# Gated linear-attention and local-attention block: KV^T in two 64-column array tiles, W2 = KV·Wo in 32x32 array tiles

## The chip, the cores and the metric

One NeuronCore of one Trainium2 chip. The metric is the device time of one execution in microseconds (us), median over several executions. PE is TensorE, PEld its loads of weights, DVE is VectorE, ACT is ScalarE, SP is SyncE, and PSUM is the memory, in banks, that matmuls write to. The chain of a profile is the work that ended last, followed back step by step to what each step had waited for.

## The reference, cut to what matters

```python
# S = 2048 tokens, D = 1024, H = 32 heads of Dh = 32; everything bf16
g = sigmoid((x * gate_w).sum(-1, keepdims=True))
# branch A, linear attention
q, k, v = split_heads(x @ A_wqkv)
pq, pk  = phi(q), phi(k)                       # phi(t) = where(t > 0, t + 1, exp(t)) + 1e-6
kv  = einsum("bhsd,bhse->bhde", pk, v)         # one 32x32 matrix per head
z   = pk.sum(over s)
num = einsum("bhqd,bhde->bhqe", pq, kv)
o   = num / (einsum("bhqd,bhd->bhq", pq, z)[..., None] + 1e-6)
a   = merge_heads(o) @ A_wo
# branch B: dilated local attention with its own weights, cut
return g * a + (1 - g) * b
```

Only the block-diagonal part of the 1024x1024 matrix KV is wanted: 32 blocks of 32x32, one per head. Since `a` is linear in `kv`, the kernel multiplies KV into Wo once (it calls the product W2), and then needs one matmul chain per row tile instead of two.

## The kernel before

Stages, with their matmuls on PE: pk = phi(x Wk) (`pk_ps`); G = x^T pk (`g_ps`); KV^T = Wv^T G (`kv_ps`); W2 = KV Wo, interleaved with V of branch B (both `p_ps`); V and q of branch A, row tile by row tile ("V/qA stage"); k and q of branch B with the local attention in between (`kq_ps`, `s`, `oB`); output (`d_ps`).

The parts that the change touches (cuts marked):

```python
# bdmask: 128x128, ones in the four diagonal 32x32 blocks
for c in range(KT):                              # 8 chunks of 128 columns = 4 heads each
    kvp = ps_1.tile([P, P], F32, name="kv_ps", tag="p1")
    for kt in range(KT):
        nc.tensor.matmul(kvp[:], lhsT=WvA[c // 4][:, kt, (c % 4) * P:(c % 4 + 1) * P],
                         rhs=G[c // 4][:, kt, (c % 4) * P:(c % 4 + 1) * P],
                         start=(kt == 0), stop=(kt == KT - 1))
    nc.vector.tensor_tensor(out=KVT[:, c, :], in0=kvp[:], in1=bdmask[:], op=ALU.mult)
# ...
def w2_event(c):                                 # two full-array matmuls per chunk
    def go():
        for half in range(2):
            w2p = bank1()                        # one of six PSUM banks
            nc.tensor.matmul(w2p[:], lhsT=KVT[:, c, :], rhs=WoA[half][:, c, :], start=True, stop=True)
            if half:
                nc.scalar.copy(out=WoA[half][:, c, :], in_=w2p[:])
            else:
                nc.vector.tensor_copy(out=WoA[half][:, c, :], in_=w2p[:])
    return go
# ... the end of normalize(t, pq, pn, prod), once per row tile of 128 tokens:
nc.vector.tensor_scalar(out=den[:], in0=den[:], scalar1=1e-6, scalar2=None, op0=ALU.add)
nc.vector.reciprocal(out=den[:], in_=den[:])
nc.vector.scalar_tensor_tensor(                  # pn = pq * ratio * (1/den), 1024 columns
    out=pn.rearrange("p (h e) -> p h e", h=H), in0=pq.rearrange("p (h e) -> p h e", h=H),
    scalar=ratio[:, t:t + 1], in1=den[:].rearrange("p (h o) -> p h o", o=1).broadcast_to([P, H, Dh]),
    op0=ALU.mult, op1=ALU.mult)
# ... V matmuls of the first four row tiles, with the W2 pairs put between them:
units = [u for t in range(4) for u in v_units(t)]
interleave(units, [(4 + 8 * c, w2_event(c)) for c in range(KT)])
```

Of each 128x128 product `kvp` only the four diagonal 32x32 blocks are used, a quarter; and in W2 three quarters of each weight matrix are zeros.

The softmax here doesn't subtract the row's maximum and nothing guards it: scores larger than these inputs give would overflow.

Of the kernel before, what the change touches and what calls it, by code (L numbers as in the profile page):

```python
# [9 lines left out]
ALU = mybir.AluOpType  # L10
BF16 = mybir.dt.bfloat16
F32 = mybir.dt.float32
PE = mybir.EngineType.PE
DVE = mybir.EngineType.DVE
P = 128
# [14 lines left out]
def interleave(units, events):  # L30

    events = sorted(events, key=lambda e: e[0])
    for i, unit in enumerate(units):
        while events and events[0][0] <= i:
            events.pop(0)[1]()
        unit()
    for _, fn in events:
        fn()
# [3 lines left out]
def kernel(  # L42
# [11 lines left out]
    nc = tc.nc  # L54
    S, D = A_x.shape[1:]
# [8 lines left out]
    H = 32  # L64
    Dh = D // H
    KT = D // P
# [5 lines left out]
    consts = ctx.enter_context(tc.tile_pool(name="consts", bufs=1))  # L72
    wpool = ctx.enter_context(tc.tile_pool(name="wpool", bufs=2))
# [5 lines left out]
    def load_w(name, src, col0, tag, only=(0, 1)):  # L79
        halves = []  # L80
        for h in only:
            w = wpool.tile([P, KT, 512], BF16, name=f"{name}{h}", tag=tag)
            c0 = col0 + h * 512
            nc.sync.dma_start(out=w[:], in_=src[:, c0:c0 + 512].rearrange("(kt p) n -> p kt n", p=P))
            halves.append(w)
        return halves
# [9 lines left out]
    for i in range(4):  # L96
        if i == 2:
            nc.sync.dma_start_transpose(out=xT[:, :, P:2 * P], in_=rows(x, P, 2 * P))
        nc.sync.dma_start(out=WkA[0][:, 2 * i:2 * i + 2, :],  # L99
                          in_=A_wqkv[2 * i * P:(2 * i + 2) * P, D:D + 512].rearrange("(kt p) n -> p kt n", p=P))  # L100
# [6 lines left out]
    WvA = load_w("WvA", A_wqkv, 2 * D, "wb")  # L107
    WoA = load_w("WoA", A_wo, 0, "wo")
# [3 lines left out]

    onesb = consts.tile([P, P], BF16, name="onesb")
    nc.vector.memset(onesb[:], 1.0)
    bdmask = consts.tile([P, P], F32, name="bdmask")
    nc.vector.memset(bdmask[:], 0.0)
    for i in range(4):
        nc.vector.memset(bdmask[32 * i:32 * i + 32, 32 * i:32 * i + 32], 1.0)


    def band(dst, lead):
# [11 lines left out]
    ratio = consts.tile([P, NB], F32, name="ratio")  # L133
    omg = consts.tile([P, NB], F32, name="omg")
    zrow = consts.tile([P, D], F32, name="zrow")
    KVT = consts.tile([P, KT, P], BF16, name="KVT")

    work = ctx.enter_context(tc.tile_pool(name="work", bufs=3))
    small3 = ctx.enter_context(tc.tile_pool(name="small3", bufs=2))
# [1 line left out]
    def phi(dst, pj):  # L141
        e = work.tile([P, 512], F32, name="e", tag="e")
        nc.scalar.activation(out=e[:], in_=pj[:], func=ACT.Exp)  # L143
        nc.vector.tensor_scalar(out=e[:], in0=e[:], scalar1=1.0, scalar2=1e-6, op0=ALU.min, op1=ALU.add)  # L144
        nc.vector.scalar_tensor_tensor(out=dst, in0=pj[:], scalar=0.0, in1=e[:], op0=ALU.max, op1=ALU.add)

    with tc.manual_schedule(engines={PE}):

        with ExitStack() as s1:
            ps_1 = s1.enter_context(tc.tile_pool(name="ps_1", bufs=6, space=bass.MemoryType.PSUM))  # L150
# [37 lines left out]
            for t in range(1, NB):  # L188
                side.append(lambda t=t: nc.vector.tensor_tensor(
                    out=zacc[:], in0=zacc[:] if t > 1 else pk[:, 0, :], in1=pk[:, t, :], op=ALU.add))  # L190
            side.append(lambda: nc.gpsimd.partition_all_reduce(zrow[:], zacc[:], P, bass_isa.ReduceOp.add))
            for t in range(NB):
                side.append(lambda t=t: nc.vector.tensor_tensor_reduce(
                    out=gjunk[:], in0=xrow[:, t, :], in1=gw_row[:], scale=1.0, scalar=0.0, op0=ALU.mult,
                    op1=ALU.add, accum_out=gdot[:, t:t + 1]))

            G = []
            for half in range(2):
                g_ = kq.tile([P, KT, 512], BF16, name=f"G{half}", tag="kq")
                G.append(g_)  # L200
                for kt in range(KT):
                    pj = ps_1.tile([P, 512], F32, name="g_ps", tag="p1")
                    for t in range(NB):
                        nc.tensor.matmul(pj[:], lhsT=xrow[:, t, kt * P:(kt + 1) * P],  # L204
                                         rhs=pk[:, t, half * 512:(half + 1) * 512],
                                         start=(t == 0), stop=(t == NB - 1))
# [7 lines left out]
            nc.vector.tensor_scalar(out=omg[:], in0=ratio[:], scalar1=1.0, scalar2=None, op0=ALU.add)  # L214
            nc.vector.reciprocal(out=omg[:], in_=omg[:])

            for c in range(KT):
                kvp = ps_1.tile([P, P], F32, name="kv_ps", tag="p1")
                for kt in range(KT):
                    nc.tensor.matmul(kvp[:], lhsT=WvA[c // 4][:, kt, (c % 4) * P:(c % 4 + 1) * P],  # L220
                                     rhs=G[c // 4][:, kt, (c % 4) * P:(c % 4 + 1) * P],
                                     start=(kt == 0), stop=(kt == KT - 1))
                nc.vector.tensor_tensor(out=KVT[:, c, :], in0=kvp[:], in1=bdmask[:], op=ALU.mult)
            WkB = load_w("WkB", B_wqkv, D, "wb")


# [9 lines left out]
            def bank1():  # L236
                return ps_1.tile([P, 512], F32, name="p1_ps", tag="p1")

            def w2_event(c):
                def go():  # L240
                    for half in range(2):
                        w2p = bank1()
                        nc.tensor.matmul(w2p[:], lhsT=KVT[:, c, :], rhs=WoA[half][:, c, :], start=True, stop=True)  # L243
                        if half:
                            nc.scalar.copy(out=WoA[half][:, c, :], in_=w2p[:])
                        else:
                            nc.vector.tensor_copy(out=WoA[half][:, c, :], in_=w2p[:])
                return go

            def v_units(t):  # L250
                def mm(half, kt, st):
                    if kt == 0:
                        st["pj"] = bank1()
                    nc.tensor.matmul(st["pj"][:], lhsT=xT[:, kt, t * P:(t + 1) * P], rhs=WvB[half][:, kt, :],  # L254
                                     start=(kt == 0), stop=(kt == KT - 1))
                    if kt < KT - 1:
                        return
                    v = Vst[t % 2]
                    nc.scalar.copy(out=v[:, half * 16:(half + 1) * 16, 0:Dh],
                                   in_=st["pj"][:].rearrange("p (h e) -> p h e", h=16))  # L260
                    if half == 1:
                        par, j = divmod(t, 8)

                        n = 128 - 16 * j
                        nc.sync.dma_start(out=V[16 * j:128, par * 9 + j], in_=v[0:n])
                        nc.sync.dma_start(out=V[0:16 * (j + 1), par * 9 + j + 1], in_=v[128 - 16 * (j + 1):128])
                for half in range(2):
                    st = {}
                    for kt in range(KT):
                        yield lambda half=half, kt=kt, st=st: mm(half, kt, st)  # L270

            def normalize(t, pq, pn, prod):
                nc.vector.tensor_tensor(out=prod, in0=pq, in1=zrow[:], op=ALU.mult)
                den = small3.tile([P, H], F32, name="den", tag="den")
                nc.vector.tensor_reduce(out=den[:], in_=prod.rearrange("p (h e) -> p h e", h=H),
                                        axis=mybir.AxisListType.X, op=ALU.add)
                nc.vector.tensor_scalar(out=den[:], in0=den[:], scalar1=1e-6, scalar2=None, op0=ALU.add)
                nc.vector.reciprocal(out=den[:], in_=den[:])
                nc.vector.scalar_tensor_tensor(
                    out=pn.rearrange("p (h e) -> p h e", h=H), in0=pq.rearrange("p (h e) -> p h e", h=H),  # L280
                    scalar=ratio[:, t:t + 1], in1=den[:].rearrange("p (h o) -> p h o", o=1).broadcast_to([P, H, Dh]),
                    op0=ALU.mult, op1=ALU.mult)

            def qa_units(t, bank, evacuate):
                def mm(half, kt, st):
# [11 lines left out]
            def qa_finish(t, half, pj):  # L297
                pq, pn = tmp[:, 4 + t % 2, :], tmp[:, 6 + t % 2, :]
                phi(pq[:, half * 512:(half + 1) * 512], pj)
                if half == 1:  # L300
                    normalize(t, pq, pn, prods[t % 2])
                    nc.sync.dma_start(out=pqd[t * P:(t + 1) * P, :], in_=pn)

            units = [u for t in range(4) for u in v_units(t)]
            interleave(units, [(4 + 8 * c, w2_event(c)) for c in range(KT)])
            for t in range(12):
                for u in v_units(4 + t):
                    u()
# [5 lines left out]
        with ExitStack() as s2:  # L314
# [102 lines left out]
            WoB = load_w("WoB", B_wo, 0, "wb")  # L417
            raw = wpool.tile([P, 4, D], BF16, name="raw", tag="wc")
            fw = wpool.tile([P, 2, D], F32, name="fw", tag="wc")
            pqT = [kq.tile([P, KT, 512], BF16, name="pqT0", tag="kq")]  # L420
            for t in range(4):
                nc.sync.dma_start_transpose(out=pqT[0][:, :, t * P:(t + 1) * P], in_=pqd[t * P:(t + 1) * P, :])
# [4 lines left out]
            def qa_late(t):  # L427
                r = raw[:, t - 12, :]
                for half in range(2):
                    h = slice(half * 512, (half + 1) * 512)  # L430
                    phi(r[:, h], r[:, h])
                normalize(t, r, r, fw[:, t % 2, :])
                nc.sync.dma_start_transpose(out=pqT[1][:, :, (t - 4) * P:(t - 3) * P], in_=r)

            def out_units(tb, bank):
                def mm(c0, n, side, c, st):
# [72 lines left out]
```

## Time and profile before

| | before |
|---|---|
| time, median of 3 runs | 491.4 us (491.37 to 491.46) |
| PE busy | 484.8 of 490.9 us |
| DVE busy | 279.1 us |
| KV^T and W2 on the chain | 3.57 and 3.45 us |

The page of the profile: busy time of the engines, and the chain of waits that ended last, by engine.

```profile
PE 484.8 (99%) x3332; PEld 230.5 (47%) x3332; DVE 279.1 (57%) x512; ACT 188.4 (38%) x283; POOL 16.0 (3%) x33
...
PE 98%; DMA 1%; SPq 0%; ACT 0%; issue 0%; ACTq 0%
```

So PE is what everything waits for, and only PE time counts unless another engine starts to hold it back. The next fence is that chain in order of time: start in us, length in us, engine, tile and line, and how many instructions were merged.

```profile
7.99 56.25 PE pk_ps L156 x252
64.24 55.25 PE g_ps L204 x256
119.49 3.57 PE kv_ps L220 x64
123.07 0.86 PE p_ps L254 x4
123.93 0.43 PE p_ps L243 x2
124.36 1.73 PE p_ps L254 x8
...
223.21 14.46 PE kq_ps L331 x67
```

Read three things here. KV^T (L220) is 64 matmuls in 3.57 us, 55.8 ns each. W2 (L243) is a pair of 512-column matmuls in 0.43 us, 216 ns each, eight times over: 3.45 us. And the next 512-column matmul always starts when the last one's column stream ends. From the start of KV^T to the first `kq_ps` matmul are 223.21 - 119.49 = 103.72 us; I call this **the stretch**: everything the change touches on PE before the output stage lies in it.

DVE in the V/qA stage, from the timeline (start, length, engine, line, operation, count, and in brackets the idle time before it and who ended it):

```profile
152.28 1.28 DVE L279 SCALAR_TENSOR_TENSOR tmp<-tmp,ratio,den 128x1024 bf16<-128x1024 bf16 x1
153.49 0.42 DVE L144 TENSOR_SCALAR e<-e 128x512 f32<-128x512 f32 x1
153.94 0.69 DVE L145 SCALAR_TENSOR_TENSOR tmp<-p_ps,e 128x512 bf16<-128x512 f32 x1
154.81 0.43 DVE L144 TENSOR_SCALAR e<-e 128x512 f32<-128x512 f32 x1 [0.18 <-ACT e L143]
```

L279 takes 1.21 us from its start to the next start, and there is one idle gap of about 0.2 us in each row tile of 6.9 us: DVE is nearly as full as PE in this stage.

### The profile page before, as it was taken

The page shows a single profiled execution, that of the slowest core. Times are in us where ns is not written, and L with a number is a line of the kernel's source. Part 1 is how long each engine was busy: PE and PEld are TensorE (multiplying, and loading weights), DVE is VectorE, ACT ScalarE, POOL GpSimd, SP SyncE. Part 2 cuts the span into 40 slices and gives each one's busy share as a digit, 9 for nine tenths or more (in the row PEclk, how much of TensorE's full clock was granted, in tenths as well). Part 3 has the DMA queues.
Part 4 walks back from the last instruction along what each step waited for, and adds up shares of the span by engine and source line. Part 5 has one row for each costly group of instructions (what it writes and reads, how often), then busy time and mean ns, then how long its engine had stood idle before and what let it go on. Part 6 is the DMA issues. An engine that isn't in the chain of part 4 may idle for free.

```text
span 490.9 us, 8143 instructions
## 1 busy us (share of the span) xinstructions
PE 484.8 (99%) x3332; PEld 230.5 (47%) x3332; DVE 279.1 (57%) x512; ACT 188.4 (38%) x283; POOL 16.0 (3%) x33
## 2 busy tenths in 40 slices
PE   7999999999999999999999999999999999999997
PEld 4444444446444444444445444445545444444444
DVE  0766689993328999997366666656655596000000
ACT  1333311111443333332566665666664332212121
POOL 3000000402000000000000000000000000000000
PEclk8999999999999999999999999999999999999999
DMA  8999960000621222236011151111163953111111
GB/s 193 153 276 371 348 224 0 0 1 5 216 62 61 91 95 88 63 125 196 3 30 37 32 115 30 30 36 29 37 151 81 212 87 85 33 43 33 43 34 43
DMA packets 80181, 46.56 MB, mean 95 GB/s; under 512 B 53520, under 2 KB 74128, under 8 KB 80144
## 3 DMA queue, kind: packets, MB, share of 16 engines
q1 hardware_dynamic: 80144, 46.04, 35.4%
q8 instruction: 26, 0.43, 0.4%
q14 instruction: 11, 0.09, 0.1%
HBM read 21.23 MB, written 7.34 MB: 58 GB/s over the span
## 4 chain that ended last, share of the span: by engine, by line
PE 98%; DMA 1%; SPq 0%; ACT 0%; issue 0%; ACTq 0%
PE kq_ps L331 23%; PE d_ps L444 21%; PE pk_ps L156 11%; PE g_ps L204 11%; PE p_ps L254 11%; PE p_ps L288 8%; PE q_ps L288 3%; PE oB L382 3%; PE s L357 2%; PE q_ps L444 1%; DMA xT<-in_A_x_dram 1%; PE kv_ps L220 1%; PE p_ps L243 1%; SPq L95 0%; SPq L99 0%; ACT osb L449 0%
## 5 line engine op out<-in xcount | busy, mean ns | idle before, releaser
L367 ACT ACTIVATE PT<-s 128x896 bf16<-128x896 f32 (+1 forms) x72 | 63.0, 926 | 24.5 <-PE s L357 24.5
L331 PE MATMUL kq_ps<-xT,WkB 128*128 128x512 bf16 x256 | 65.3, 379 | 0.0
L331 PE MATMUL kq_ps<-xT,WqB 128*128 128x512 bf16 x256 | 64.8, 379 | 0.0
L368 DVE TENSOR_TENSOR PT<-PT,mask 128x896 bf16<-128x896 bf16 (+1 forms) x72 | 44.7, 624 | 26.6 <-ACT PT L367 26.5
L156 PE MATMUL pk_ps<-WkA,xT 128*128 128x512 bf16 x256 | 57.4, 387 | 1.7 <-DMA WkA<-in_A_wqkv_dram 0.9
L254 PE MATMUL p_ps<-WvB,xT 128*128 128x512 bf16 x256 | 58.5, 379 | 0.0
L444 PE MATMUL d_ps<-WoA,pqT 128*128 128x512 bf16 (+1 forms) x248 | 56.9, 372 | 0.0
L444 PE MATMUL d_ps<-WoB,OBT 128*128 128x512 bf16 (+1 forms) x248 | 56.9, 372 | 0.0
L204 PE MATMUL g_ps<-pk,xrow 128*128 128x512 bf16 x256 | 55.4, 379 | 0.0
L144 DVE TENSOR_SCALAR e<-e 128x512 f32<-128x512 f32 x64 | 27.2, 425 | 43.5 <-ACT e L143 43.5
L449 ACT ACTIVATE osb<-d_ps,omg 128x512 bf16<-128x512 f32 (+1 forms) x31 | 20.9, 674 | 76.2 <-PE d_ps L444 76.1
L288 PE MATMUL p_ps<-WqA,xT 128*128 128x512 bf16 x192 | 43.4, 379 | 0.0
L156 PEld LDWEIGHTS <-xT 128*128 128x128 bf16 x256 | 25.5, 100 | 33.5 <-issue 3.5
L336 ACT CAST kqt<-kq_ps 128x512 bf16<-128x512 f32 x48 | 28.2, 588 | 31.8 <-PE kq_ps L331 31.6
L444 PEld LDWEIGHTS <-pqT 128*128 128x128 bf16 x264 | 25.8, 98 | 29.5
L444 PEld LDWEIGHTS <-OBT 128*128 128x128 bf16 x264 | 25.8, 98 | 29.3
L204 PEld LDWEIGHTS <-xrow 128*128 128x128 bf16 x256 | 25.0, 98 | 30.2
L254 PEld LDWEIGHTS <-xT 128*128 128x128 bf16 x256 | 25.0, 98 | 30.0
L288 PEld LDWEIGHTS <-xT 128*128 128x128 bf16 x256 | 24.3, 98 | 28.5
L143 ACT ACTIVATE e<-pk_ps 128x512 f32<-128x512 f32 x32 | 19.0, 597 | 43.8 <-PE pk_ps L156 43.8
L331 PEld LDWEIGHTS <-WqB 128*128 128x128 bf16 x256 | 23.0, 97 | 24.7
L331 PEld LDWEIGHTS <-WkB 128*128 128x128 bf16 x256 | 22.6, 97 | 24.1
(57 smaller groups left out, 400.3 us busy)
## 6 DMA issues: line engine op xcount, KB each, us to landing
xrow<-in_A_x_dram SPq DMA_DIRECT2D x4, 1024.0 KB, 12.7
out_dram<-osb SPq DMA_DIRECT2D x31, 128.0 KB, 1.9
pqd<-tmp SPq DMA_DIRECT2D x12, 256.0 KB, 2.1
WvA<-in_A_wqkv_dram SPq DMA_DIRECT2D x2, 1024.0 KB, 16.6
WoA<-in_A_wo_dram SPq DMA_DIRECT2D x2, 1024.0 KB, 13.7
WvB<-in_B_wqkv_dram SPq DMA_DIRECT2D x2, 1024.0 KB, 11.9
WqA<-in_A_wqkv_dram SPq DMA_DIRECT2D x2, 1024.0 KB, 10.0
WkB<-in_B_wqkv_dram SPq DMA_DIRECT2D x2, 1024.0 KB, 7.4
```

What stands on the lines that cost most here:

```text
L143: nc.scalar.activation(out=e[:], in_=pj[:], func=ACT.Exp)
L144: nc.vector.tensor_scalar(out=e[:], in0=e[:], scalar1=1.0, scalar2=1e-6, op0=ALU.min, op1=ALU.add)
L156: nc.tensor.matmul(pj[:], lhsT=xT[:, kt, t * P:(t + 1) * P], rhs=WkA[half][:, kt, :], start=(kt == 0), stop=(kt == KT - 1))
L204: nc.tensor.matmul(pj[:], lhsT=xrow[:, t, kt * P:(kt + 1) * P], rhs=pk[:, t, half * 512:(half + 1) * 512], start=(t == 0), stop=(t == NB - 1))
L254: nc.tensor.matmul(st["pj"][:], lhsT=xT[:, kt, t * P:(t + 1) * P], rhs=WvB[half][:, kt, :], start=(kt == 0), stop=(kt == KT - 1))
L288: nc.tensor.matmul(st["pj"][:], lhsT=xT[:, kt, t * P:(t + 1) * P], rhs=WqA[half][:, kt, :], start=(kt == 0), stop=(kt == KT - 1))
L331: nc.tensor.matmul(st["pj"][:], lhsT=W[c // 4][:, kt, (c % 4) * P:(c % 4 + 1) * P], rhs=xT[:, kt, cols], start=(kt == 0), stop=(kt == KT - 1))
L336: (nc.vector.tensor_copy if 0 <= after < 4 else nc.scalar.copy)(out=kqt[:, which, cols], in_=st["pj"][:])
L367: nc.scalar.activation(out=ptv[:, hs], in_=s4[:, hs, 0:W_], func=ACT.Exp, scale=SCALE)
L368: nc.vector.tensor_tensor(out=ptv[:, hs], in0=ptv[:, hs], in1=m[:, None, :].broadcast_to([P, 2, W_]), op=ALU.mult)
L444: nc.tensor.matmul(st["ps"][:, 0:n], lhsT=lhsT, rhs=W[c0 // 512][:, c, c0 % 512:c0 % 512 + n], start=(side == 0 and c == 0), stop=(side == ...
L449: nc.scalar.activation(out=osb[:, 0:n], in_=st["ps"][:, 0:n], func=ACT.Copy, scale=omg[:, tb:tb + 1])
```

## The change

The intent: use the array as several small ones, so that less of it works on blocks that are thrown away. KV^T is computed in two column tiles of 64 (two heads each), and no mask is needed. W2 is computed in passes of 16 matmuls, one per 32x32 tile of the array, each with 32 rows, 32 columns and a 512-column stream; row tile r writes to PSUM bank r, column tile j to its partitions 32j. So bank r of a pass gets head r of each of four chunks. The rows of W2 thus come out with the heads transposed within groups of four chunks, and `normalize` has to write `pn` in the same order.

```diff
-    KVT = consts.tile([P, KT, P], BF16, name="KVT")
+    KVT = consts.tile([P, KT, 64], BF16, name="KVT")
@@ KV^T
-            for c in range(KT):
-                kvp = ps_1.tile([P, P], F32, name="kv_ps", tag="p1")
-                ...  (64 matmuls of 128 columns, mask multiply)
+            for g in range(2):
+                kvp = ps_1.tile([P, 4, 64], F32, name="kv_ps", tag="p1")
+                for c in range(4):
+                    for kt in range(KT):
+                        for j in range(2):
+                            cols = slice(c * P + 64 * j, c * P + 64 * j + 64)
+                            nc.tensor.matmul(kvp[64 * j:64 * j + 64, c, :], lhsT=WvA[g][:, kt, cols],
+                                             rhs=G[g][:, kt, cols], start=(kt == 0), stop=(kt == KT - 1))
+                nc.vector.tensor_copy(out=KVT[:, 4 * g:4 * g + 4, :], in_=kvp[:])
@@ W2
-            def w2_event(c):  ...
+            def w2_event(g, half):
+                def go():
+                    w2p = [bank1() for _ in range(4)]
+                    for j in range(4):
+                        for r in range(4):
+                            rs = slice(32 * r, 32 * r + 32)
+                            nc.tensor.matmul(w2p[r][32 * j:32 * j + 32, :],
+                                             lhsT=KVT[rs, 4 * g + j, (r % 2) * 32:(r % 2) * 32 + 32],
+                                             rhs=WoA[half][rs, 4 * g + j, :], start=True, stop=True)
+                    for r in range(4):
+                        (nc.scalar.copy if r % 2 else nc.vector.tensor_copy)(
+                            out=WoA[half][:, 4 * g + r, :], in_=w2p[r][:])
@@ normalize
-                nc.vector.scalar_tensor_tensor(  ... 1024 columns, times ratio and 1/den)
+                nc.vector.tensor_scalar(out=den[:], in0=den[:], scalar1=ratio[:, t:t + 1], scalar2=None, op0=ALU.mult)
+                for g in range(2):
+                    nc.vector.tensor_tensor(
+                        out=pn[:, 512 * g:512 * g + 512].rearrange("p (r j e) -> p j r e", r=4, j=4),
+                        in0=pq[:, 512 * g:512 * g + 512].rearrange("p (j r e) -> p j r e", r=4, j=4),
+                        in1=den[...].broadcast_to([P, 4, 4, Dh]), op=ALU.mult)
@@ placing the passes
-            interleave(units, [(4 + 8 * c, w2_event(c)) for c in range(KT)])
+            interleave(units, [(8 + 12 * (2 * g + half), w2_event(g, half)) for g in range(2) for half in range(2)])
@@ (cut: the mask is gone; the four late row tiles write pn to a tile of their own instead of in place)
```

More of the change, by code (lines that the diff above doesn't have):

```diff
@@ L114 @@
     nc.vector.memset(onesb[:], 1.0)
-    bdmask = consts.tile([P, P], F32, name="bdmask")
-    nc.vector.memset(bdmask[:], 0.0)
-    for i in range(4):
-        nc.vector.memset(bdmask[32 * i:32 * i + 32, 32 * i:32 * i + 32], 1.0)
     def band(dst, lead):
@@ L215 @@
             nc.vector.reciprocal(out=omg[:], in_=omg[:])
-            for c in range(KT):
-                kvp = ps_1.tile([P, P], F32, name="kv_ps", tag="p1")
-                for kt in range(KT):
-                    nc.tensor.matmul(kvp[:], lhsT=WvA[c // 4][:, kt, (c % 4) * P:(c % 4 + 1) * P],
-                                     rhs=G[c // 4][:, kt, (c % 4) * P:(c % 4 + 1) * P],
-                                     start=(kt == 0), stop=(kt == KT - 1))
-                nc.vector.tensor_tensor(out=KVT[:, c, :], in0=kvp[:], in1=bdmask[:], op=ALU.mult)
+            for g in range(2):
[7 more added lines that the diff above has]
+                nc.vector.tensor_copy(out=KVT[:, 4 * g:4 * g + 4, :], in_=kvp[:])
             WkB = load_w("WkB", B_wqkv, D, "wb")
@@ L237, in bank1 @@
                 return ps_1.tile([P, 512], F32, name="p1_ps", tag="p1")
-            def w2_event(c):
+            def w2_event(g, half):
                 def go():
-                    for half in range(2):
-                        w2p = bank1()
-                        nc.tensor.matmul(w2p[:], lhsT=KVT[:, c, :], rhs=WoA[half][:, c, :], start=True, stop=True)
-                        if half:
-                            nc.scalar.copy(out=WoA[half][:, c, :], in_=w2p[:])
-                        else:
-                            nc.vector.tensor_copy(out=WoA[half][:, c, :], in_=w2p[:])
+                    w2p = [bank1() for _ in range(4)]
[8 more added lines that the diff above has]
+                            out=WoA[half][:, 4 * g + r, :], in_=w2p[r][:])
                 return go
@@ L278, in normalize @@
                 nc.vector.reciprocal(out=den[:], in_=den[:])
-                nc.vector.scalar_tensor_tensor(
-                    out=pn.rearrange("p (h e) -> p h e", h=H), in0=pq.rearrange("p (h e) -> p h e", h=H),
-                    scalar=ratio[:, t:t + 1], in1=den[:].rearrange("p (h o) -> p h o", o=1).broadcast_to([P, H, Dh]),
-                    op0=ALU.mult, op1=ALU.mult)
+                nc.vector.tensor_scalar(out=den[:], in0=den[:], scalar1=ratio[:, t:t + 1], scalar2=None, op0=ALU.mult)
[3 more added lines that the diff above has]
+                        in0=pq[:, 512 * g:512 * g + 512].rearrange("p (j r e) -> p j r e", r=4, j=4),
+                        in1=den[:, 16 * g:16 * g + 16].rearrange("p (j r o) -> p j r o", r=4, o=1)
+                        .broadcast_to([P, 4, 4, Dh]), op=ALU.mult)
             def qa_units(t, bank, evacuate):
@@ L419 @@
             fw = wpool.tile([P, 2, D], F32, name="fw", tag="wc")
+            lw = wpool.tile([P, 4, D], BF16, name="lw", tag="wa")
             pqT = [kq.tile([P, KT, 512], BF16, name="pqT0", tag="kq")]
@@ L431, in qa_late @@
                     phi(r[:, h], r[:, h])
-                normalize(t, r, r, fw[:, t % 2, :])
-                nc.sync.dma_start_transpose(out=pqT[1][:, :, (t - 4) * P:(t - 3) * P], in_=r)
+                pn = lw[:, t - 12, :]
+                normalize(t, r, pn, fw[:, t % 2, :])
+                nc.sync.dma_start_transpose(out=pqT[1][:, :, (t - 4) * P:(t - 3) * P], in_=pn)
             def out_units(tb, bank):
```

## The prediction

> **What bounds the kernel.** TensorE. The page shows PE busy 485 of 491 us, and the chain that ended last is 98% PE: in it one 512-column matmul follows the next every 0.216 us (16 in 3.45 us) without a gap from 8 us on. So the time changes by what the PE stream loses or gains, unless another engine starts to hold PE back.
>
> **What the change touches on PE.** KV^T: 64 matmuls of 128 columns, 3.57 us (chain, 119.5 to 123.1). W2: 16 matmuls of 512 columns, eight pairs of 0.43 us, 3.45 us (chain, 123.9 to 139.5). Together 7.0 us, 1.4% of the span, all on the chain: the ceiling of any gain.
>
> **After, estimated.**
> - W2: 4 passes of 16 matmuls on 32x32 tiles. Nearest in the trace is the scores group (32x128, four row tiles, 16 matmuls of 112 columns): 0.31 us in the chain for 16 x 47 ns of streaming, so four tiles do run at once; about 0.1 us of gap on each side I read as the cost of changing the tile mode. "TensorEngine Tiling (Array Packing)", Key Properties, says that changing the mode drains the engine, and that different tiles work in parallel. A pass then takes one stream (0.21 us), 15 issue steps of 5 to 15 ns and 0.2 us of switching: 0.5 to 0.6 us. Four: 2.1 us, a gain of 1.3 us.
> - KV^T: 128 matmuls of 64 columns in two column tiles: half the work, twice the instructions. The trace's small matmuls run at 20 ns (scores) to 25 ns (oB, 33 columns) each, weight load included: 128 at 20 to 27 ns is 2.6 to 3.5 us, plus a switch. The tiling page says that column tiling gives up fast weight load. [...]128 one after another 3.5 us. I take 3.2 us: a gain of 0.3 us, possibly a loss.
> - Sum: 7.0 to 5.3 us.
>
> **DVE.** normalize exchanges one 1.285 us operation (1.21 start to start) for a small scaling (0.2 us) and two 512-column multiplies of about 0.69 us each (estimate from 1.225 us for 1024 columns): +0.35 us for each of 16 row tiles. In the V/qA stage DVE idles only 0.2 us in each 6.9 us row tile (timeline), so it falls behind PE by about 0.15 us a row tile and ends the stage 1 to 2 us later. Six PSUM banks cover that, and its next work is 2.4 us later: PE should not notice. The four late row tiles run where DVE is mostly idle. The KVT copies are off the chain. The four banks of a pass are evacuated (2 x 0.69 DVE, 2 x 0.59 ACT, one V evacuation) within the 2.6 us to the next pass.
>
> **Prediction: 489.8 us, 488.8 to 491.6 (8 in 10).** Faster by over 2%: 1%. Within 2%: 98%. Slower: 1%.
>
> **What would show it.** In the chain: KV^T at 2.6 to 3.5 us; four W2 passes of 0.5 to 0.6 us; all later stages as long as before, 1 to 2 us earlier. On DVE: a new group of about 0.69 us, x32, and under 0.1 us of idle per row tile in the V/qA stage. No new PE wait on DVE or ACT.
>
> **What would make it wrong.** Column-tile weight loads that neither overlap nor run at the assumed rate (50 ns each: 6.4 us for KV^T, no gain, total about 493). The 16 tiles of a pass not running at once (four waves: 0.9 us a pass, no gain). The 4-dimensional multiply running slower than a plain one, so that DVE lags by more than the banks hold. A wait for banks at the passes.

## The result, and the profile after

| | before | after |
|---|---|---|
| time, median of 6 runs each | 491.38 us (490.72 to 492.78) | 488.53 us (487.95 to 489.80) |
| the stretch, from the chains | 103.72 us | 100.82 us |
| PE busy | 484.8 us | 480.5 us |
| DVE busy | 279.1 us | 281.0 us |

The ratio of the times is 0.9943, 95% interval 0.9924 to 0.9962 (the mean time of one kernel's fast runs over that of the other's of the same rounds, so not quite the ratio of the medians quoted). The gain of 2.85 us between the medians is clear of noise. The range ended at 488.8; the median lies 0.27 us below it. The prediction was wrong on the good side. That miss is small beside the spread of single runs (487.95 to 489.80 us); what shows that the sum behind the prediction was off is the stretch, 2.90 us shorter where 1.6 us had been predicted.

The chain after, the same columns:

```profile
8.69 53.74 PE pk_ps L152 x248
62.43 55.25 PE g_ps L200 x256
117.69 2.15 PE kv_ps L220 x128
119.83 1.83 PE p_ps L258 x8
121.66 0.36 PE p_ps L246 x16
122.03 2.70 PE p_ps L258 x12
...
218.51 14.46 PE kq_ps L339 x67
```

KV^T is down from 3.57 to 2.15 us although it has twice as many matmuls. A W2 pass takes 0.36 us for 16 matmuls, and there are four instead of eight pairs of 0.43. The V matmuls beside them (L258) became slightly longer: 8 take 1.83 us instead of 1.73, 12 take 2.70 instead of 2.59 (12 x 0.216). That is where a change of tile mode shows: about 0.11 us at each return to the full array. Going in costs nearly as much: by the single starts in the trace, 0.309 us lie between the last V matmul and the first tile of a pass, where the next full-array matmul would follow after 0.216. This 0.09 us is part of the 0.36 us of a pass. The whole account of the stretch: KV^T gains 1.42 us; from the end of KV^T to the first q matmul of branch A, 20.72 us (123.07 to 143.79) became 19.26 (119.83 to 139.09), 1.46 us less; together 2.88, and the stretch is 2.90 us shorter. What comes after is the same in both.

A warning about comparing the two spans: 490.9 and 486.2 us differ by 4.7, not by 2.9. The other 1.8 us lie before KV^T, in code that PE runs alike in both kernels: `g_ps` starts at 64.24 us in the one profile and at 62.43 in the other. Two experiments below that share this beginning with the changed kernel (kv_four32_split and kv_onetile) started `g_ps` at 62.33 and 64.34 us. The run of before that was profiled took 492.63 us, 1.25 above its kernel's median, and that of after 487.95 us, 0.58 below. So it is the chance of the start (in the slices of the page, the first slice of before had a granted clock of 8 tenths, after had 9), and part of the spread of about 2 us among the runs of one kernel. This is why I argue from the stretch and not from the span.

The groups of KV^T and W2 after, from the list of groups by line and shape (line, engine, operation, output<-inputs, shapes, count | busy us, mean ns of one | idle before):

```profile
L220 PE MATMUL kv_ps<-G,WvA 128*64 128x64 bf16 x128 | 2.2, 196 | 0.0
L246 PE MATMUL p_ps<-WoA,KVT 32*32 32x512 bf16 x64 | 1.7, 385 | 0.0
```

The length of one matmul (196 or 385 ns) is its latency, not its cost. The cost is the group's time in the chain over its count: 128 matmuls with their loads in 2.15 us are 16.8 ns each, or 33.6 ns for a pair, the change of mode at the start included. In the timeline a W2 pass is busy 0.43 us with matmuls of 0.385 us, so the 16 starts lie within 0.045 us: 3 ns apart. All 16 tiles stream at the same time. The Trainium skill, "TensorE: Matmul & The Clock Gate", Measured speedup vs the span model, gives about 4 ns per tile for this; the trace agrees.

DVE in the same place of the V/qA stage after:

```profile
154.43 0.24 DVE L284 TENSOR_SCALAR den<-den,ratio 128x32 f32<-128x32 f32 x1
154.70 1.29 DVE L286 TENSOR_TENSOR tmp<-tmp,den 128x512 bf16<-128x512 bf16 x2
155.91 0.42 DVE L140 TENSOR_SCALAR e<-e 128x512 f32<-128x512 f32 x1
156.37 0.69 DVE L141 SCALAR_TENSOR_TENSOR tmp<-p_ps,e 128x512 bf16<-128x512 f32 x1
157.02 0.43 DVE L140 TENSOR_SCALAR e<-e 128x512 f32<-128x512 f32 x1
```

The two multiplies of 512 columns take 1.21 us from start to next start, exactly as much as the one operation of 1024 columns before; the new cost is the small scaling, 0.27 us from start to start (154.43 to 154.70). The idle gap of 0.18 us is gone. DVE's last multiply of the stage ended 6.25 us after the first `kq_ps` matmul before (229.46 against 223.21), and 6.54 us after it now (225.05 against 218.51).

### The profile page after: what moved, and what is told of

Read it like the earlier page. It is cut to its first block, busy times and chain, and to the rows that moved or that the text cites. A ratio compares the mean times of both kernels' runs of the same rounds, so it can differ in the third digit from the quotient of the medians.

```text
span 486.2 us, 8390 instructions
## 1 busy us (share of the span) xinstructions
PE 480.5 (99%) x3444; PEld 227.0 (47%) x3444; DVE 281.0 (58%) x533; ACT 187.4 (39%) x283; POOL 15.9 (3%) x33
## 4 chain that ended last, share of the span: by engine, by line
PE 98%; DMA 1%; SPq 1%; ACT 0%; issue 0%; ACTq 0%
PE kq_ps L339 23%; PE d_ps L454 21%; PE p_ps L258 11%; PE g_ps L200 11%; PE pk_ps L152 11%; PE p_ps L296 9%; PE q_ps L296 3%; PE oB L390 3%; PE s L365 2%; PE q_ps L454 1%; DMA WkA<-in_A_wqkv_dram 1%; PE kv_ps L220 0%; PE p_ps L246 0%; SPq L95 0%; SPq L98 0%; SPq L99 0%
## 5 line engine op out<-in xcount | busy, mean ns | idle before, releaser
L258 PE MATMUL p_ps<-WvB,xT 128*128 128x512 bf16 x256 | 57.9, 379 | 0.0
L152 PE MATMUL pk_ps<-WkA,xT 128*128 128x512 bf16 x256 | 56.0, 379 | 1.3 <-DMA WkA<-in_A_wqkv_dram 0.8
L459 ACT ACTIVATE osb<-d_ps,omg 128x512 bf16<-128x512 f32 (+1 forms) x31 | 20.9, 673 | 76.5 <-PE d_ps L454 73.7
L152 PEld LDWEIGHTS <-xT 128*128 128x128 bf16 x256 | 24.9, 98 | 32.2 <-issue 1.6
L258 PEld LDWEIGHTS <-xT 128*128 128x128 bf16 x256 | 24.6, 98 | 30.0 <-issue 0.9
L296 PEld LDWEIGHTS <-xT 128*128 128x128 bf16 x256 | 24.3, 98 | 28.5
```

Source lines behind the costliest of these rows:

```text
L152: nc.tensor.matmul(pj[:], lhsT=xT[:, kt, t * P:(t + 1) * P], rhs=WkA[half][:, kt, :], start=(kt == 0), stop=(kt == KT - 1))
L258: nc.tensor.matmul(st["pj"][:], lhsT=xT[:, kt, t * P:(t + 1) * P], rhs=WvB[half][:, kt, :], start=(kt == 0), stop=(kt == KT - 1))
L296: nc.tensor.matmul(st["pj"][:], lhsT=xT[:, kt, t * P:(t + 1) * P], rhs=WqA[half][:, kt, :], start=(kt == 0), stop=(kt == KT - 1))
L459: nc.scalar.activation(out=osb[:, 0:n], in_=st["ps"][:, 0:n], func=ACT.Copy, scale=omg[:, tb:tb + 1])
```

## The experiments

Twelve kernels were run. The theory after the result: **A**, the gain is the sum of two independent parts on PE, KV^T and W2; KV^T is faster than predicted because the two column tiles load and stream at the same time. Rivals: **B**, most of the gain is W2 and the KV^T group only looks short; **C**, a matmul of 64 columns is simply cheap, whatever tile it is on; **D**, DVE holds PE back or releases it.

### The parts alone: kv_only, w2_only, norm_only, after_again

kv_only, KV^T alone, on the kernel before:

```diff
+    nc.vector.memset(KVT[:], 0.0)
@@ KV^T as in the change, but evacuated into the 128-wide block-diagonal KVT of before
+                for j in range(2):
+                    js = slice(64 * j, 64 * j + 64)
+                    nc.vector.tensor_tensor(out=KVT[js, 4 * g:4 * g + 4, js], in0=kvp[js],
+                                            in1=bdmask[js, None, js].broadcast_to([64, 4, 64]), op=ALU.mult)
```

> Undoes W2 and normalize, keeps the two 64-column tiles for KV^T (the block diagonal is cut out by the mask while evacuating). Theory A (the gain is the sum of two independent parts on PE): the KV^T group takes 2.15 us as in the changed kernel instead of 3.57, the stretch from the first KV^T matmul to the first kq_ps matmul is 1.4 us shorter than before (103.7 to 102.3), time about 490.0. Theory B (the gain is mostly W2, KV^T only looks short in the trace): the stretch stays within 0.5 us of 103.7.

w2_only, the changed kernel with the old KV^T:

```diff
@@ the 64 matmuls of 128 columns of before, then
+                for j in range(2):
+                    js = slice(64 * j, 64 * j + 64)
+                    nc.vector.tensor_copy(out=KVT[js, c, :], in_=kvp[js, js])
```

> Keeps the old 128x128 KV^T matmuls (3.57 us), with the new W2 passes and the new normalize. Theory A: each of the four passes costs 0.36 us plus about 0.12 us in the matmuls around it, the stretch from the first KV^T matmul to the first kq_ps matmul is 1.46 us shorter than before (103.7 to 102.3), time about 490.0. Theory B: about 2.4 us or more shorter.

norm_only, the new `normalize` (and the separate output tile of the late row tiles) put into the kernel before; nothing else.

> The new normalize (and its separate output tile) alone on the kernel before; the result is wrong on purpose, since the heads are transposed and W2 does not follow. DVE gets about 0.27 us more in each 6.9 us row tile. Theory A: PE does not notice, the stretch from KV^T to kq_ps stays at 103.7 us within 0.1 and the time is 491.4 within noise. Rival (DVE holds PE back): some us longer.

after_again is the changed kernel, unedited.

> The changed kernel again, as a control on the same chip: 2.85 us less than before in time (within 0.6), and 100.8 us from the first KV^T matmul to the first kq_ps matmul. If the 1.8 us that its first profile gained before the KV^T group (62.4 against 64.2 us at the start of g_ps) is chance, that start is not earlier in every profile.

Measured, on one chip, with the kernel before at 490.95 us (11 runs):

| kernel | time, 6 runs | ratio to before (95%) | stretch | against 103.72 |
|---|---|---|---|---|
| kv_only | 489.91 us | 0.9977 (0.9961 to 0.9994) | 102.40 us | -1.32 |
| w2_only | 489.99 us | 0.9977 (0.9960 to 0.9995) | 102.15 us | -1.57 |
| norm_only | 491.83 us | 1.0010 (0.9992 to 1.0028) | 103.72 us | 0.00 |
| after_again | 487.76 us | 0.9935 (0.9920 to 0.9951) | 100.82 us | -2.90 |

All but norm_only gave the reference's result. The chain of kv_only:

```profile
117.54 2.15 PE kv_ps L224 x128
119.68 0.97 PE p_ps L260 x4
...
219.94 14.46 PE kq_ps L337 x67
```

The chain of w2_only:

```profile
117.79 3.57 PE kv_ps L217 x64
121.36 1.73 PE p_ps L258 x8
123.09 0.37 PE p_ps L246 x16
...
219.94 14.46 PE kq_ps L339 x67
```

The chain of norm_only:

```profile
118.58 3.57 PE kv_ps L220 x64
...
222.30 14.46 PE kq_ps L334 x67
```

The parts add up: 1.32 + 1.57 = 2.89. Rival B falls: KV^T alone is worth nearly as much as W2. In kv_only the four V matmuls after KV^T take 0.97 us instead of 0.86, the 0.11 us of the change of mode; that is why 1.42 us in the group become 1.32 in the stretch, and it is also the 0.10 us by which the first V group of the changed kernel is longer, which I had booked to W2 above. Rival D falls for this change: `normalize` alone moves the stretch by nothing. The times of single kernels spread by about 2 us, so by times alone kv_only and w2_only are only just distinguishable from before.

### Why is a KV^T matmul so cheap: kv_serial, kv_full, kv_n32, kv_onetile

kv_serial: the two column tiles no longer alternate.

```diff
-                    for kt in range(KT):
-                        for j in range(2):
+                    for j in range(2):
+                        for kt in range(KT):
```

> The changed kernel with the two column tiles of KV^T no longer alternating: for each chunk all eight contraction steps of tile 0, then all eight of tile 1. Same 128 instructions. Theory A (the 16.8 ns per load and matmul come from two column tiles loading and streaming at the same time): consecutive matmuls now hit the same tile, so each costs one tile's own period, 27 to 34 ns, and the group takes 3.5 to 4.3 us instead of 2.15. Rival B (a 64-column load and matmul simply costs 17 ns, whichever tile): 2.15 us.

kv_full: the whole array as weights, 64 columns streamed, half of the output rows thrown away; two banks.

```diff
+                            nc.tensor.matmul(kvp[j][:, c, :], lhsT=WvA[g][:, kt, c * P:(c + 1) * P],
+                                             rhs=G[g][:, kt, cols], start=(kt == 0), stop=(kt == KT - 1))
```

> KV^T with 128 matmuls of 64 columns on the whole array (128-column weights, half of the rows of each result thrown away), no tiles. Theory A: no overlap of tiles, so 128 matmuls at 64 columns cost about 27 to 29 ns each (estimate: half of the 55.8 ns that the 128-column matmul took), 3.5 to 3.7 us. Rival B (fewer columns per matmul alone gives the gain): about 2.15 us.

kv_n32: 64-column weights as in the change, but only 32 columns streamed (the result is wrong).

> The changed kernel with only 32 of the 64 moving columns in each KV^T matmul, 64-column weights as before; the result is wrong on purpose. If a tile's period is set by its weight load, or by the issue of instructions, the group stays at 2.1 us; if it is set by the streaming of the 64 columns[...], it falls to about 1.3 us.

kv_onetile: the changed kernel's 128 matmuls, all on column tile 0.

```diff
-                            nc.tensor.matmul(kvp[64 * j:64 * j + 64, c, :], lhsT=WvA[g][:, kt, cols],
+                            nc.tensor.matmul(kvp[j][0:64, c, :], lhsT=WvA[g][:, kt, cols],
@@ and each half moved to its partitions by the copy
+                    nc.vector.tensor_copy(out=KVT[64 * j:64 * j + 64, 4 * g:4 * g + 4, :], in_=kvp[j][0:64])
```

> KV^T with the same 128 loads and matmuls (64 columns each), but all on the first column tile, into two banks; the second half is moved to its partitions when it is evacuated, so the result stays correct. In kv_serial tile 1 may still have started while tile 0 had matmuls waiting. If the 16.8 ns per matmul of the changed kernel needs the second tile: each matmul then costs one tile's own step, about 27 ns, the group 3.5 us. If not: about 2.2 to 2.7 us.

The KV^T line of the chain of each, in the order kv_serial, kv_full, kv_n32, kv_onetile:

```profile
117.86 2.67 PE kv_ps L220 x128
```

```profile
118.72 3.73 PE kv_ps L220 x128
```

```profile
117.47 2.13 PE kv_ps L221 x128
```

```profile
119.59 4.17 PE kv_ps L220 x128
```

| kernel (once each) | KV^T | per matmul | stretch | time |
|---|---|---|---|---|
| changed kernel, two tiles alternating | 2.15 us | 16.8 ns | 100.82 us | 487.76 us (median of 6) |
| kv_onetile, one tile | 4.17 us | 32.6 ns | 102.85 us | 491.86 us |
| kv_full, whole array | 3.73 us | 29.1 ns | 102.31 us | 490.45 us |
| kv_serial, one tile after the other | 2.67 us | 20.9 ns | 101.35 us | 488.62 us |
| kv_n32, half the stream | 2.13 us | 16.6 ns | 100.82 us | 487.71 us |

Only kv_n32 differed from the reference. kv_onetile began KV^T about 1.9 us later than the changed kernel (119.59 against 117.69 us); that is in its time, but not in its stretch. What follows:

- kv_onetile decides. One tile needs 32.6 ns for each load and matmul, somewhat more than the 27 ns expected; two tiles in turn need 33.6 ns for a **pair**. The second tile is as good as free. Rival C falls, and kv_full says the same in another way: 64-column matmuls on the whole array cost 29.1 ns each, so halving the columns alone would have gained nothing over the 3.57 us of before. Both kernels also write to two banks in turn, which the changed kernel does not. That is not what slows them: kv_serial's first matmuls, all on tile 0 and in one bank, start 31 to 32 ns apart (after a first gap of 53 ns), as they do in kv_onetile. And in the changed kernel the two matmuls of a pair start 3 ns apart, and the pairs 32 ns apart (single starts in the packed traces).
- kv_n32: half the stream changes nothing (2.13 us). So the 33 ns are not the streaming of 64 columns. They go with what stayed the same, the loading of 64 columns of weights and the tile's own turnaround; the run does not separate these two.
- kv_serial missed its expectation of 3.5 to 4.3 us: 20.9 ns is less than the 32.6 ns that one tile needs. So tile 1 must work beside tile 0 even when the program lists eight matmuls of one and then eight of the other. The single starts fit this: they read as series of eight, 31 to 32 ns apart, and a new series begins 5 to 6 ns after the fifth start of the one before it. (The trace does not name the tile of a matmul; this is read from the pattern.) Alternating is better, by 0.5 us, but not necessary for most of the overlap.

### More and smaller tiles: kv_four32 and kv_four32_split

If two column tiles overlap, four might too, and with 32 columns only the wanted blocks are computed. kv_four32:

```diff
-                        for j in range(2):
-                            cols = slice(c * P + 64 * j, c * P + 64 * j + 64)
-                            nc.tensor.matmul(kvp[64 * j:64 * j + 64, c, :], lhsT=WvA[g][:, kt, cols],
+                        for j in range(4):
+                            cols = slice(c * P + 32 * j, c * P + 32 * j + 32)
+                            nc.tensor.matmul(kvp[32 * j:32 * j + 32, c, :], lhsT=WvA[g][:, kt, cols],
```

> KV^T in four 32-column tiles, only the 32x32 diagonal blocks: 256 matmuls of 32 columns, correct result, KVT half as wide. If four tiles overlap as two do and only a tile's own load and stream count: 64 rounds of about 20 ns, 1.3 us, the kernel 0.85 us faster than the changed one, about 487.3 (at best a tie in time, shown by the trace). If there is a floor per instruction of 8 ns or more: 2.1 us or longer, no gain.

It was correct, and no gain: 491.01 us (6 runs, before 490.97 on the same chip; ratio 1.0005, 0.9987 to 1.0023), stretch 103.13 us. (The stretch is 2.3 us longer than that of the changed kernel, the median time 3.2 us; how long the pause was in the runs without a profile is not known.) Its chain:

```profile
117.90 1.65 PE kv_ps L220 x187
119.54 2.11 issue
121.65 0.70 PE kv_ps L220 x69
```

Two things went wrong. The 256 matmuls take 1.65 + 0.70 = 2.35 us, 9.2 ns each, so 37 ns for four tiles where I had hoped for 20. By the single starts, the first 32 matmuls run in rounds of four, about 25 ns a round after the first; from then on they start 8 to 9 ns apart, one by one, as in the other case that the expectation had named. What runs out there is not known. And in the middle PE stands still for 2.11 us, waiting for nothing that the profile shows ("issue"). In that window the DMA view has this row for 118 to 124 us, in kv_four32:

```profile
q8 instruction: 2, 0.03, 2.1%
```

and in the changed kernel for 117 to 124 us:

```profile
q8 instruction: 1, 0.02, 0.8%
```

These are blocks of instructions being fetched, 16 KB each. In the `g_ps` stage of kv_four32, where a matmul with its load comes every 0.216 us, one such fetch follows the other after 27.7 us, the time of 128 matmuls and 128 loads: so this queue feeds PE. In the trace of kv_four32 the first of the two starts at 119.30 us, 0.24 us before the pause; PE goes on at 121.65 us. The Trainium skill, "Runtime: NRT & Kernel Launch", Instruction fetch mechanics, says that each engine refills its instruction memory in blocks of 16 KiB, 256 instructions, and calls the cost mostly hidden. 256 matmuls with 256 loads are two such blocks, used up here in 2.35 us. So the theory: PE ran out of instructions. kv_four32_split puts eight V matmuls between the two halves:

```diff
-            for g in range(2): ...
+            def kv_group(g): ...
+            kv_group(0)
@@ second half after 8 V matmuls, the W2 passes 4 matmuls later than in the change
+            interleave(units, [(8, second_group)] + [(12 + 12 * (2 * g + half), w2_event(g, half)) for g in range(2) for half in range(2)])
```

> kv_four32 with its two halves (128 matmuls each) apart: eight V matmuls stand between them. kv_four32 stood still for 2.1 us in the middle of its 256 matmuls, 0.25 us after the fetch of one 16 KB block of instructions had begun. If PE had run out of instructions there: no such pause, and the two halves take 0.8 to 1.1 us each, 1.6 to 2.1 us together. If the pause belongs to something else in KV^T (the G or WvA tiles, the bank, the mode): it stays near 2 us.

Its chain:

```profile
117.58 1.12 PE kv_ps L220 x128
118.71 1.83 PE p_ps L258 x8
120.54 0.48 PE kv_ps L220 x51
121.03 0.37 issue
121.40 0.77 PE kv_ps L220 x77
```

The pause shrank from 2.11 to 0.37 us, with the same tiles, banks and matmuls, only thinned out; the halves take 1.12 and 1.25 us (a little over the expectation). (The edit also puts the load of WkB behind the second half, but it was issued at nearly the same time, 118.79 against 119.11 us.) Two numbers of the traces bind the pause to the fetch. PE stops after 187 matmuls counted from the start of KV^T in both kernels (128 + 8 + 51 in this one), so after as many instructions, though at another matmul of KV^T. And it goes on 2.35 us after the fetch began in kv_four32 (119.30 to 121.65) and 2.34 us in this one (119.06 to 121.40). The block itself had landed after 0.92 and 0.97 us; what the rest is spent on is not shown. This supports the instruction supply as the cause, and goes against the tiles, the bank or the mode; a direct record of PE waiting for its instructions is not in the trace, so I call it supported, not shown. One run, 488.55 us, correct: no better than the changed kernel, since 2.37 us of KV^T plus the pause is more than 2.15 (stretch 101.54 us against 100.82). So neither four-tile version beats the changed kernel.

### What a W2 pass costs: w2_split

Each pass is cut into two visits of 8 tiles (two of the four chunks), with four V matmuls between; same 64 matmuls.

```diff
-                    for j in range(4):
+                    for j in (2 * part, 2 * part + 1):
@@ copies after the second part; events at 8 + 12 * pass + 4 * part
```

> Each W2 pass of 16 tiles cut into two visits of 8 tiles with four V matmuls between. If a visit costs one 512-column stream plus the change of mode, however many of the 16 tiles it uses: eight visits of about 0.34 us plus 0.12 us, 3.7 us instead of 2.0, and the stretch from KV^T to kq_ps grows by about 1.7 us to 102.5. If the cost goes by matmuls: half per visit, no change (100.8).

Its chain:

```profile
121.97 0.34 PE p_ps L250 x8
122.30 0.97 PE p_ps L264 x4
```

A visit of 8 matmuls takes 0.34 us, one of 16 takes 0.36, and each return costs 0.11 us beside it. The stretch is 102.50 us (117.99 to 220.49), 1.68 us longer for four more visits, as expected. A pass costs its 512-column stream plus the change of mode, and the other tiles come nearly free. The run gave 489.92 us, once.

### How far is DVE from holding PE back: norm_heavy

The first product of `normalize` is done twice:

```diff
                 nc.vector.tensor_tensor(out=prod, in0=pq, in1=zrow[:], op=ALU.mult)
+                nc.vector.tensor_tensor(out=prod, in0=pq, in1=zrow[:], op=ALU.mult)
```

> The changed kernel with the first product of normalize done twice: 1.26 us more of DVE in each row tile, so that DVE needs about 8.1 us of work for 6.9 us of PE. It tests the claim that six banks cover a small lag of DVE and how far: after 12 row tiles DVE is about 14 us behind; the banks hold about 5 to 8 us. Expected: the V/qA stage (from the first W2 pass to the first kq_ps matmul) stretches by 6 to 10 us and the time rises to 494 to 499. If DVE did not matter at all for PE, 488.

The time was 495.06 us (once, correct), within the 494 to 499 expected, but not where I had put it, and partly by chance: its KV^T began at 119.32 us, 1.6 us later than in after_again (117.74). PE in the timeline:

```profile
217.98 3.61 PE L297 MATMUL p_ps<-WqA,xT 128*128 128x512 bf16 x16 [1.03 <-DVE tmp L141]
```

The first listed idle time of PE on DVE is 1.03 us before the last q group (by the starts, 0.26 us was lost at the q group before it); the whole stretch grew only by about 1.5 us, and the rest of the loss fell in the next stage, where `kq_ps` waited once for ACT (2.2 us) and once for DVE (1.5 us) by the view of who waited for whom. The banks and the end of the stage took up more lag than my 5 to 8 us. So the small extra DVE work of the change has room, as norm_only shows, but 1.26 us per row tile has not.

## Why the prediction was right or wrong

The prediction was wrong in size: 489.8 (488.8 to 491.6) against 488.53 us measured. Point by point:

1. **PE bounds the kernel, 7.0 us are the ceiling.** Right: the chain after is again 98% PE, and the gain in the stretch is 2.90 us.
2. **W2: "Four: 2.1 us, a gain of 1.3 us".** Nearly right. By w2_only the gain is 1.57 us, so W2 costs 3.45 - 1.57 = 1.88 us, 0.47 us a pass with its changes of mode, against the 0.5 to 0.6 predicted. The Trainium skill, "TensorEngine Tiling (Array Packing)", Key Properties, says that tiles work in parallel and that a change of mode drains the engine; the trace agrees with the first (3 ns between starts), and 0.09 us on going in and 0.11 us at a return fit the second.
3. **KV^T: "128 at 20 to 27 ns is 2.6 to 3.5 us", "128 one after another 3.5 us. I take 3.2 us".** This is the step that failed. The loads do not come one after another: they and the matmuls of the two column tiles run side by side, at 33.6 ns a pair (16.8 ns each), while one tile alone needs 32.6 ns for each (kv_onetile). The group took 2.15 us. The mis-sized term: 3.2 us against 2.15 us in the group, or 2.25 us with its return to the full array. Of the 1.3 us between the predicted gain (491.4 - 489.8 = 1.6) and the measured stretch (2.90), this term is about 1.0; W2 gives another 0.2, and the rest is rounding. I had cited that different tiles work in parallel, used it for W2, and then added up KV^T as if there were one tile; the lower bound of 20 ns came from a group of the trace that has no column tiles. A clause cut from the prediction read the weight loads of that group (the scores, on four row tiles) as 14 ns apart. That is busy time over count, 0.22 us over 16; the single starts lie 2 to 4 ns apart within each four. So loads that run side by side could already be seen in the trace of before. Whether column tiles give up fast weight load, as the prediction cites, no run here isolates.
4. **DVE "falls behind PE by about 0.15 us a row tile and ends the stage 1 to 2 us later".** Wrong in size, right in effect. The extra work was 0.27 us per row tile, not 0.35, because two multiplies of 512 columns cost 1.21 us start to start, as the one operation did; it filled the idle gap, and DVE ended the stage only 0.3 us later relative to PE. PE did not notice (norm_only: 0.00 us).
5. **"No new PE wait on DVE or ACT".** Right: no PE group of the changed kernel in the stretch shows idle time, and the waits for banks did not come.
6. **The range.** It reached down to a gain of 2.6 us. The two PE terms with their lower costs as I had bounded them (2.6 us for KV^T, 0.5 us a pass) would have given 7.0 - 4.6 = 2.4 us; the range ended where those bounds did, and the bound on KV^T was taken from groups of another shape.

## What to carry to other kernels

When a small matmul group is costed for array tiles, cost one round over all tiles (the load and turnaround of one tile), not the sum over the instructions, and add about 0.1 us for each change of mode, going in as well as coming back (0.09 and 0.11 us here). Collect as many tiles as possible into one visit, since a visit costs its stream whether 8 or 16 tiles use it. But do not cut further once the instructions, not the columns, are what is used up: four tiles of 32 columns doubled the instructions and lost what the two tiles of 64 had gained, most of it in one pause of 2.11 us.

## What the Trainium skill lacked or had wrong

- "TensorE: Matmul & The Clock Gate", Part 3: Packing small matmuls — row/col tiling, says in one point that a weight load overlaps with matmuls in flight only when its rows differ. The two column tiles of KV^T use the same rows, and still a pair costs 33.6 ns where one tile alone costs 32.6 ns for each. "TensorEngine Tiling (Array Packing)", Key Properties, has it right.
- "TensorE: Matmul & The Clock Gate", Wait — 56ns, not 53.3ns?, says that start to start never drops below about 25 ns. Alternating column tiles ran at 16.8 ns per load and matmul, four 32-column tiles at 9.2 ns outside the pause, and the 16 tiles of a W2 pass start 3 ns apart. A single column tile (32.6 ns) stays above that floor, and the whole array meets it: the 33-column matmuls of `oB` take about 25 ns each in the chain of before (16 in 0.39 to 0.40 us).
- No page read here gives the time that one column tile needs for a load and a short matmul in turn: 32.6 ns for 64 columns, and not shorter when only 32 columns are streamed with two tiles in turn (33.3 ns a pair).
- "TensorEngine Tiling (Array Packing)", Key Properties, names the drain at a change of mode without a figure. Here the first tile of a pass started 0.09 us later than a full-array matmul would have, and the matmuls after a return to the full array took about 0.11 us longer.
- "Runtime: NRT & Kernel Launch", Instruction fetch mechanics, calls the fetch of instructions mostly hidden. A run of 512 short PE instructions stood still for 2.11 us beside such a fetch, and 0.37 us when it was thinned out; that the fetch is the cause is supported (PE went on 2.35 and 2.34 us after it began), not shown.
